# Nine matmuls of ones in TensorE's order for each of the first three pairs of attention tiles

## The chip, the cores and the metric

The kernel runs on one core of one Trainium2 chip. The metric is the device time of one execution in microseconds (us); the median over runs is what two kernels are compared by.

## The reference, cut to what matters

Pooled attention over 2 batches of 8 heads, then two feed-forward blocks on the 1152 tokens that come out. Inputs and outputs are float32.

```python
q_pool = q.reshape(B, H, S // 2, 2, D).mean(axis=3)           # B, H, S, D = 2, 8, 1152, 64
scores = (1 / sqrt(D)) * q_pool @ k^T
attn = exp(scores - max); attn = attn / (sum(attn) + 1e-9)
x = attn @ v                                                   # reshaped to 1152 x 512
h = x @ w_in;  g = P(h) / (Q(h) + 1e-6);  x = g @ w_out        # w_in 512 x 2048
xn = rms_norm(x) * rms_g
out = (silu(xn @ w_gate) * (xn @ w_val)) @ w_out2              # w_gate, w_val 512 x 1536
```

## The kernel before, in words

**Attention** goes by pairs of heads. A pair of heads has nine tiles of 128 pooled queries (four of the first head, one that holds the last 64 queries of both, four of the second head); the eight pairs of heads make 72 tiles. For one tile, QK is the score matmuls of line 783 into three PSUM banks of `hid`, in two pieces, AB (banks 0 and 1) and C (bank 2). DVE takes the negated row maximum (line 812), ACT the exponentials with their sums (line 818), PE turns them (line 834) back into the same banks, piece T and, once the copy of bank 0 has left, piece T2; ACT and DVE copy the turned tile into `pt` (lines 866 and 869). When all tiles of a head are there, PE multiplies `pt` with the values (line 938, into `av`). There are two sets of banks, one for even tiles and one for odd ones, so QK of a tile waits until the tile two before it has been copied out.

**What comes beside it.** For each head, K and the pooled Q (the sum of line 674, on POOL or DVE) are turned on PE (line 732, into `prep`) and copied to `kT` and `qT` (lines 616 and 619). When a pair of heads is finished, its rows are divided by their sums (lines 989 and 994) and split into a rounded part `x_hi` (lines 616 or 619) and a rest `x_lo` (line 632). During attention the float64 weights of the first feed-forward block are also loaded and turned into float32 pairs: the first nine stay in SBUF (lines 175 to 208), the later ones, here called spills, go through ACT (175, 215), DVE (180, 223) and POOL (219, 232, 236) and back to DRAM.

**The order on PE** is written out in `attention()`, in the list `seq`. It takes tiles two by two: AB and C of both, then up to five value products of earlier tiles, then T of both, then T2 of the first. Each entry of `seq` depends on the one before it. The value products come from `av_ops`; the first of them carries the number 4 (the tile that completes the first head), and one is taken only in turns with a larger tile number, so the turns of tiles 0 and 1, 2 and 3, 4 and 5 have none.

**The order elsewhere** comes from a planner, `order()`. It holds a list of operations with costs in nanoseconds, buffers and due times, steps through a modelled time, and for each engine picks among what is ready; an operation that has several ways (a copy by ACT or DVE, a sum by POOL or DVE) gets the one that ends first by the model. The instructions are issued in the order that comes out, and at run time they wait for each other by semaphores. SP issues all DMAs, in one queue.

**Before the first QK**, `f_warm` issues nine matmuls of `ones` by `ones` (line 1015).

The feed-forward blocks follow (the matmuls of line 525). Their first two units of hidden features are projected while attention ends, and the rational function of the first block (lines 1125 to 1176) reads the projections out of the same `hid` banks: a bank set is free again when DVE has done line 1134 for it.

Of the kernel before, what the change touches and what calls it, by code (L numbers as in the profile page):

```python
# [8 lines left out]
F32 = mybir.dt.float32  # L9
# [5 lines left out]
PSUM = bass.MemoryType.PSUM  # L15
# [4 lines left out]
def attention_moe_moe2_kernel(  # L20
# [18 lines left out]
    nc = tc.nc  # L39
# [19 lines left out]
    def pool(tag, bufs=1, space=None):  # L59
        if tag not in pools:  # L60
            kw = {} if space is None else {"space": space}
            pools[tag] = scope[-1].enter_context(tc.tile_pool(name=tag, bufs=bufs, **kw))
# [3 lines left out]
    def T(tag, shape, dtype=F32, space=None):  # L66
        pool(tag, BUFS.get(tag, 1), space)
        return pools[tag].tile(shape, dtype, tag=tag, name=tag)
# [5 lines left out]
    ones = T("ones", [128, 128])  # L74
# [369 lines left out]
    PE, DVE, ACT, POOL = "PE", "DVE", "ACT", "POOL"  # L444
# [89 lines left out]
    def banked(accesses, g, ins, also=None):  # L534

        ins = ins.ins
        for o in range(3):
            for other in accesses[o]:
                if other.engine != ins.engine:
                    if o != g and other is not also:  # L540
                        tc.declare_no_dep(ins, other, reason="another bank")
                    else:
                        tc.add_manual_dep(ins, other.name, after, reason="the same bank")
        accesses[g].append(ins)
# [64 lines left out]
    TS = 3100  # L609
# [284 lines left out]
    LAST = [NFULL, 2 * NFULL]  # L894
# [117 lines left out]
    def f_warm():  # L1012

        for _ in range(WARM):
            banked(bank[0], 0, nc.tensor.matmul(s_ps[0][:, 0, 0:128], lhsT=ones, rhs=ones, start=True, stop=True))

    WARM = 9

    tile_pe, av_ops = {}, []
    AV2 = 5  # L1020

    def attention():
        Op(PE, 213 * WARM, -1e6, f_warm)
        for i in range(len(heads)):
            head_ops(i)
        for i in range(NP * NT):
            tile_ops(i)
            if i % NT == NT - 1:
                pair_ops(i // NT)


        seq = []
        n = NP * NT
        for i in range(0, n, 2):
            a, b = tile_pe[i], tile_pe[i + 1]
            was = tile_pe.get(i - 1)
            seq += [a["AB"], *([was["T2"]] if was else []), a["C"], b["AB"], b["C"]]
            for _ in range(AV2):
                if av_ops and av_ops[0][0] < i - AVLAG:
                    seq.append(av_ops.pop(0)[1])  # L1040
            seq += [a["T"], b["T"], a["T2"]]
        seq.append(tile_pe[n - 1]["T2"])
        for x, y in zip(seq, seq[1:]):
            y.deps.append(x)

    AVLAG = 0

    attention()
    later = sum_op[0][4]
    early_h = {}  # L1050
# [475 lines left out]
```

## Time and profile before

| | us |
|---|---|
| median of 3 runs | 716.89 |
| lowest and highest run | 714.22 and 717.25 |
| the profiled execution, its own time | 718.36 |
| its span, first to last instruction | 716.6 |
| PE busy | 689.0 (96%) |
| DVE busy | 546.1 (76%) |
| ACT busy | 397.6 (55%) |
| POOL busy | 258.6 (36%) |
| mean granted clock of TensorE | 0.990 |

The span is cut into 40 slices of 17.9 us in the page's view of busy shares. Attention fills the first 15 or so (to about 278 us), the first feed-forward block the next 12, the second the rest. PE means TensorE's matmuls, DVE VectorE, ACT ScalarE, POOL GpSimdE, SP the engine that issues DMAs. A float32 matmul of the program stands as two entries in the trace, a transpose as one. [...]

### The profile page before, as it was taken

The numbers are of one execution on the slowest core, as the hardware profiler recorded it, in microseconds if no ns is written. First come the engines' busy times: TensorE is split into PE (matmuls) and PEld (weight loads), VectorE is DVE, ScalarE is ACT, GpSimd is POOL, SyncE is SP. The second block draws the span as 40 slices with busy tenths as digits, with TensorE's granted clock in tenths as the row PEclk, the third lists the DMA queues.
The fourth block names the chain that finished last, engine by engine and source line by source line (L and its number), as shares of the span: only waits on it lengthen the run. The fifth ranks groups of instructions, "written<-read, shape, count | busy, mean of one in ns | idle before, by whom it ended". The sixth has DMA issues, their size and how long they took to land.

```text
span 716.6 us, 13077 instructions
## 1 busy us (share of the span) xinstructions
PE 689.0 (96%) x5257; PEld 596.5 (83%) x5257; DVE 546.1 (76%) x721; ACT 397.6 (55%) x630; POOL 258.6 (36%) x240
## 2 busy tenths in 40 slices
PE   7999999999999999899999999998999999999997
PEld 6666666667666677899999999997999899989996
DVE  5599998989898885997996967957768156845844
ACT  4568776878877875977755655344334232402210
POOL 3022334656654465312221323255345033403500
PEclk9799999999999999999999999999999999999999
DMA  6443434765554535214105104000225112420103
GB/s 209 113 133 119 124 96 156 223 192 180 202 168 143 190 120 202 93 59 146 60 30 171 36 2 149 28 29 0 89 89 148 60 59 83 125 89 29 59 1 132
DMA packets 53900, 77.66 MB, mean 108 GB/s; under 512 B 6480, under 2 KB 36176, under 8 KB 53840
## 3 DMA queue, kind: packets, MB, share of 16 engines
q1 hardware_dynamic: 53840, 76.83, 33.3%
q8 instruction: 41, 0.67, 0.4%
q14 instruction: 19, 0.16, 0.1%
HBM read 62.40 MB, written 14.42 MB: 107 GB/s over the span
## 4 chain that ended last, share of the span: by engine, by line
PE 81%; DVE 12%; ACT 4%; issue 2%; DMA 0%; SPq 0%; DVEq 0%; ACTq 0%
PE hid L525 32%; PE accp L525 23%; PE hid L783 9%; PE av L938 9%; PE hid L834 5%; DVE nm L812 2%; DVE pt L869 2%; ACT p L818 2%; PE prep L732 2%; DVE acc L1324 1%; DVE xt L619 1%; DVE m_q L1141 1%; PE prep L985 1%; DVE wc L184 1%; DVE x_lo L1334 0%
## 5 line engine op out<-in xcount | busy, mean ns | idle before, releaser
L525 PE MATMUL hid<-x_hi,win_hi 128*128 128x384 f32 x480 | 162.3, 338 | 3.6 <-DVE m_p L1134 1.4
L525 PE MATMUL hid<-x_lo,win_hi 128*128 128x384 f32 x480 | 161.2, 336 | 0.6 <-DVE x_lo L1334 0.6
L525 PE MATMUL hid<-x_hi,win_lo 128*128 128x384 f32 x480 | 161.1, 336 | 0.0
L818 ACT ACTIVATE p<-hid,nm 128x1152 f32<-128x1152 f32 x72 | 87.9, 1222 | 28.2 <-DVE nm L812 28.0
L812 DVE TENSOR_REDUCE nm<-hid 128x1 f32<-128x1152 f32 x72 | 94.9, 1353 | 10.2 <-PE hid L783 8.9
L525 PEld LDWEIGHTS hid<-x_hi,win_hi 128*128 128x128 f32 x480 | 90.7, 189 | 6.7 <-issue 3.5
L783 PE MATMUL hid<-kT,qT 64*128 64x256 f32 (+3 forms) x800 | 95.2, 379 | 0.8 <-DVE pt L869 0.4
L1176 POOL TENSOR_TENSOR g_lo<-m_p,g_hi 128x1152 fp32r<-128x1152 f32 (+1 forms) x20 | 44.5, 2233 | 135.2 <-ACT g_hi L1173 96.8
L525 PEld LDWEIGHTS hid<-x_lo,win_hi 128*128 128x128 f32 x480 | 90.6, 189 | 1.8 <-DVE x_lo L1334 0.9
L525 PEld LDWEIGHTS hid<-x_hi,win_lo 128*128 128x128 f32 x480 | 90.5, 189 | 0.0
L834 PEld LDWEIGHTS hid<-ident,p 64*128 64x128 f32 x1296 | 53.6, 141 | 37.7 <-ACT p L818 12.3
L834 PE MATMUL hid<-ident,p 64*128 64x64 f32 x1296 | 68.5, 232 | 12.2 <-ACT p L818 7.0
L783 PEld LDWEIGHTS hid<-kT,qT 64*128 64x128 f32 (+1 forms) x800 | 70.5, 182 | 9.0 <-DVE pt L869 1.3
L938 PE MATMUL av<-pt,vn 128*64 128x288 f32 x576 | 76.7, 411 | 0.0
L866 ACT ACTIVATE pt<-hid 128x512 f32<-128x512 f32 (+2 forms) x145 | 59.7, 449 | 29.8 <-PE hid L834 29.3
L525 PE MATMUL accp<-g_hi,wout_hi 128*128 128x384 f32 x192 | 64.8, 337 | 3.0 <-ACT acc L1229 1.8
L525 PE MATMUL accp<-g_hi,wout_lo 128*128 128x384 f32 x192 | 64.2, 334 | 0.0
L525 PE MATMUL accp<-g_lo,wout_hi 128*128 128x384 f32 x192 | 64.2, 334 | 0.0
L938 PEld LDWEIGHTS av<-pt,vn 128*64 128x64 f32 x576 | 38.7, 136 | 27.1 <-issue 3.4
L175 ACT ACTIVATE wc<-wraw 128x512 f32<-128x512 f32 x68 | 45.4, 671 | 26.5 <-POOL win_lo L208 14.7
L869 DVE COPY pt<-hid 128x512 f32<-128x512 f32 (+1 forms) x79 | 47.6, 608 | 16.4 <-PE hid L834 14.9
L203 POOL TENSOR_SCALAR win_hi<-wc 128x512 fp32r<-128x512 f32 x22 | 15.2, 691 | 99.8 <-PE hid L525 90.8
(120 smaller groups left out, 1236.2 us busy)
## 6 DMA issues: line engine op xcount, KB each, us to landing
wraw<-in_moe_w_out_dram SPq DMA_DIRECT2D x28, 512.0 KB, 3.4
far<-spill SPq DMA_DIRECT2D x23, 512.0 KB, 3.3
wraw<-in_moe_w_in_dram SPq DMA_DIRECT2D x16, 512.0 KB, 3.8
wraw<-in_moe_w_gate_dram SPq DMA_DIRECT2D x12, 512.0 KB, 3.8
wraw<-in_moe_w_val_dram SPq DMA_DIRECT2D x12, 512.0 KB, 4.2
kn<-in_k_dram SPq DMA_DIRECT2D x16, 288.0 KB, 3.9
vn<-in_v_dram SPq DMA_DIRECT2D x16, 288.0 KB, 3.1
qn<-in_q_dram SPq DMA_DIRECT2D x16, 256.0 KB, 3.3
```

What stands on the lines that cost most here:

```text
L175: nc.scalar.activation(c.bitcast(F32), wt["raw", n][:, :, 1].bitcast(F32), AF.Abs, scale=2.0**-112)
L203: eng.tensor_scalar(hi, w_float(n), 1.0, 1.0, op0=ALU.mult, op1=ALU.mult)
L525: ins = nc.tensor.matmul(dst, lhsT=a[x], rhs=b[y], start=first and i == 0 and p == 0, stop=last and i == n - 1 and p == 2,)
L732: seen(nc.tensor.transpose(ps[:, at:at + 128], src, ident))
L783: ins = nc.tensor.matmul(ps[to, j, c:c + x1 - x0], lhsT=qT[2 * pr + h][rows, c0:c0 + to.stop - to.start], rhs=kT[2 * pr + h][rows, x0:x1], ...
L812: nc.vector.tensor_reduce(out=e["nm"], in_=scores(), op=ALU.max, axis=AX.X, negate=True)
L818: nc.scalar.activation(e["p"], scores(), AF.Exp, bias=e["nm"], scale=1.0, accum_out=sums[pr][:, t:t + 1])
L834: ins = nc.tensor.transpose(ps[:, g, c:c + 64], e["p"][rows, 128 * j:128 * j + 128], ident[rows, rows])
L866: return nc.scalar.activation(to, src, AF.Copy)
L869: return nc.vector.tensor_copy(to, src)
L938: nc.tensor.matmul(e["av", h][64 * c:64 * c + 64, 0:QW], lhsT=v_tile[2 * pr + h][:, KEYS[kt], :], rhs=pt[pr, h][:, kt, c * QW:(c + 1) * QW ...
L1176: eng.tensor_sub(g_(1), p_(), g_(0).bitcast(F32))
```

## The change

A function `f_fill` issues nine matmuls of `ones` by `ones` into a buffer of `av` that nobody reads. In `attention()` one such operation is put into `seq` behind C of the second tile of a turn, as long as no value product has been taken yet: that is the turns of tiles 0 and 1, 2 and 3, and 4 and 5. Its cost for the planner is 9 times 213 ns.

```diff
+    def f_fill():
+        ps = T("av", [128, 512], F32, space=PSUM)
+        for _ in range(FILL):
+            nc.tensor.matmul(ps[:, 0:128], lhsT=ones, rhs=ones, start=True, stop=True)
+
-    WARM = 9
+    WARM, FILL = 9, 9
...
             for _ in range(AV2):
                 if av_ops and av_ops[0][0] < i - AVLAG:
                     seq.append(av_ops.pop(0)[1])
+            if av_ops[0][0] == LAST[0] and len(seq) < 40 and seq[-1] is b["C"]:
+                seq.append(Op(PE, 213 * FILL, i * TS, f_fill, [], [Buf("av")]))
             seq += [a["T"], b["T"], a["T2"]]
```

The planner sees later times on PE from the first turn on, and so other engines' orders move as well. Two places follow.

The start of PE's order, first turn, as a piece of the difference (`hid` holds the scores, `av` the filling, `prep` the turned K and Q of the second head, `p` the exponentials):

```order
 L783 MATMUL hid<-kT_197,qT_213 128x256 x4
 L783 MATMUL hid<-kT_197,qT_213 128x128
+L1020 MATMUL av<-ones 128x128 x9
 L732 MATMUL prep<-ident,kn 128x128
 L732 MATMUL prep<-ident,qp 128x128 x3
```

The filling stands ahead of four transposes of the second head. The same in the second turn:

```order
 L783 MATMUL hid<-kT_197,qT_213 128x256 x4
 L783 MATMUL hid<-kT_197,qT_213 128x128
+L1020 MATMUL av<-ones 128x128 x9
 L834 MATMUL hid<-ident,p 128x64 x35
 L783 MATMUL hid<-kT_197,qT_213 64x256
```

Here it stands directly ahead of the turning of tiles 2 and 3; in the third turn it stands ahead of four transposes of the third head.

DVE in the same stretch, before (`pt` is the turned tile, `nm` the negated maximum, `qp` the pooled query of a head):

```order
L619 TENSOR_SCALAR kT_232<-prep 128x128
L619 TENSOR_SCALAR qT_277<-prep 128x384
L869 COPY pt<-hid 128x8x64
L619 TENSOR_SCALAR qT_277<-prep 128x256
L869 COPY pt<-hid 128x8x64
L812 TENSOR_REDUCE nm<-hid 128x1 x2
```

and with the change:

```order
L619 TENSOR_SCALAR kT_232<-prep 128x128
L619 TENSOR_SCALAR qT_309<-prep 128x384
L869 COPY pt<-hid 128x8x64
L619 TENSOR_SCALAR qT_309<-prep 128x256
L674 TENSOR_TENSOR qp<-qn_153 128x640
L869 COPY pt<-hid 128x8x64
L812 TENSOR_REDUCE nm<-hid 128x1 x2
```

The sum that makes the fourth head's pooled query has come from POOL's queue into DVE's, ahead of the copy of tile 1 and of the maxima of tiles 2 and 3.

The end of attention on DVE, before (`xt` is the last pair of heads' result, `m_q` and `m_p` the first block's rational function; after the change the lines behind 1040 have numbers seven higher):

```order
L223 SCALAR_TENSOR_TENSOR wc<-wraw,wc 128x512
L989 TENSOR_TENSOR xt<-xt,prep 128x512
L619 TENSOR_SCALAR x_hi<-xt 128x576
L632 TENSOR_TENSOR x_lo<-xt,x_hi 128x576
L1141 SCALAR_TENSOR_TENSOR m_q<-m_u,absb,hid 128x384
```

and with the change:

```order
L223 SCALAR_TENSOR_TENSOR wc<-wraw,wc 128x512
L180 TENSOR_SCALAR wc<-wc 128x512
L223 SCALAR_TENSOR_TENSOR wc<-wraw,wc 128x512
L989 TENSOR_TENSOR xt<-xt,prep 128x512
L994 TENSOR_TENSOR xt<-xt,rxh 64x64 x2
L632 TENSOR_TENSOR x_lo<-xt,x_hi 128x576
L1148 SCALAR_TENSOR_TENSOR m_q<-m_u,absb,hid 128x384
```

One spill more is worked on here, the division of the last columns (line 994) has come from POOL to DVE, and `x_hi` has gone to ACT, where it stands ahead of the rational function's first operation (line 1125 before). POOL has its three operations of the additional spill (219, 232, 236) where line 994 stood. Between these two places DVE's queue takes up the first weight one turn earlier (four of its operations stand ahead of the maxima of tiles 8 and 9), and around tiles 32 to 42 the parts of the division move from DVE to POOL in one pair of heads; PE's order changes there by a few transposes that stand behind QK instead of in the midst of it.

## Rows read from the trace of the kernel before

**Rows 1.** Page, the span in 40 slices: granted clock in tenths
```profile
PEclk9799999999999999999999999999999999999999
```
**Rows 2.** Busy time by stretch, PE alone: window, its length, PE busy (entries), clock, DMA
```profile
18.20:18.40 0.20, 0.20 (x9) 0.82 0.93 282
...
28.40:28.60 0.20, 0.20 (x2) 0.58 0.00 0
```
**Rows 3.** Timeline of PE, first 30 us: start, length, operation, entries [idle before, releaser]
```profile
1.04 3.99 PE L1015 MATMUL hid<-ones 128*128 128x128 f32 x18 [1.04 <-DVE ones L75]
...
7.39 2.22 PE L783 MATMUL hid<-kT,qT 64*128 64x256 f32 x20
...
11.54 0.77 PE L834 MATMUL hid<-ident,p 64*128 64x64 f32 x17 [1.34 <-ACT p L818]
...
17.72 0.80 PE L834 MATMUL hid<-ident,p 64*128 64x64 f32 x17 [1.91 <-ACT p L818]
18.98 1.22 PE L834 MATMUL hid<-ident,p 64*128 64x64 f32 x18 [0.46 <-ACT p L818]
20.14 1.98 PE L783 MATMUL hid<-kT,qT 64*64 64x256 f32 x16
...
22.34 3.12 PE L783 MATMUL hid<-kT,qT 64*64 64x128 f32 x14
25.39 1.11 PE L732 MATMUL prep<-ident,kn 128*128 128x128 f32 x4
...
28.63 0.78 PE L834 MATMUL hid<-ident,p 64*128 64x64 f32 x18
```
**Rows 4.** Timeline of PE, a later turn with the same 14 entries
```profile
154.61 1.72 PE L783 MATMUL hid<-kT,qT 64*64 64x128 f32 x14
```
**Rows 5.** Timeline of all engines, first 20 us
```profile
5.06 0.83 DVE L674 TENSOR_TENSOR qp<-qn 128x640 f32<-128x640 f32 x1 [3.42 <-DMA qn<-in_q_dram]
...
13.63 0.69 DVE L869 COPY pt<-hid 128x512 f32<-128x512 f32 x1 [0.24 <-PE hid L834]
...
14.33 1.53 POOL L674 TENSOR_TENSOR qp<-qn 128x640 f32<-128x640 f32 x1 [1.00 <-DMA qn<-in_q_dram]
...
14.96 2.62 DVE L812 TENSOR_REDUCE nm<-hid 128x1 f32<-128x1152 f32 x2 [0.64 <-PE hid L783]
...
16.36 1.22 ACT L818 ACTIVATE p<-hid,nm 128x1152 f32<-128x1152 f32 x1 [1.39 <-DVE nm L812]
```
**Rows 6.** Timeline of DVE, maxima of tiles 8 and 9
```profile
37.68 2.62 DVE L812 TENSOR_REDUCE nm<-hid 128x1 f32<-128x1152 f32 x2
```
**Rows 7.** Timeline of DVE, POOL and PE, 124 to 130 us
```profile
125.20 1.73 DVE L632 TENSOR_TENSOR x_lo<-xt,x_hi 128x576 fp32r<-128x576 f32 x1
...
124.93 1.39 POOL L219 TENSOR_TENSOR wc<-wc,wraw 128x512 f32<-128x512 f32 x1 [6.11 <-ACT pt L866]
...
129.60 0.77 PE L834 MATMUL hid<-ident,p 64*128 64x64 f32 x17
```
**Rows 8.** Timeline of POOL, DVE and PE, end of attention
```profile
275.14 1.28 POOL L219 TENSOR_TENSOR wc<-wc,wraw 128x512 f32<-128x512 f32 x1
...
277.21 1.29 POOL L236 TENSOR_TENSOR spill<-wc,spill 128x512 fp32r<-128x512 f32 x1
...
278.56 0.69 DVE L989 TENSOR_TENSOR xt<-xt,prep 128x512 f32<-128x512 f32 x1 [4.51 <-ACT xt L616]
...
279.85 0.76 DVE L632 TENSOR_TENSOR x_lo<-xt,x_hi 128x576 fp32r<-128x576 f32 x1
280.52 0.61 DVE L1141 SCALAR_TENSOR_TENSOR m_q<-m_u,absb,hid 128x384 f32<-128x384 f32 x1
...
286.06 0.41 PE L525 MATMUL hid<-x_hi,win_hi 128*128 128x384 f32 x1 [1.42 <-DVE m_p L1134]
```
**Rows 9.** Timeline and stretches of PE, first feed-forward block
```profile
303.88 0.45 PE L525 MATMUL accp<-g_hi,wout_hi 128*128 128x384 f32 x1 [1.76 <-ACT acc L1229]
...
306.00:308.00 2.00, 2.00 (x8) 0.50 0.35 116
```

## Prediction

> **What bounds the kernel now.** I read the page's slices first. The granted clock is full everywhere but in the first slice and, far lower, in the second [rows 1]; the busy shares there show attention's first turns. A finer cut of PE's time gives the edges: the clock falls within 18.2 to 18.4 us and is back within 28.4 to 28.6 [rows 2], so some 10 us run at the lower level. What went before is in PE's timeline: PE is idle 1.34 us before tile 0 is turned and 1.91 us before tile 2 is, both times for ACT's exponentials [rows 3], because no value products stand there yet. From 18.98 us (turning of tile 3) to 28.63 (turning of tile 5) the chain of waits names PE alone: 9.65 us in which PE is what everything waits for. The same 14 matmuls cost 3.12 us there and 1.72 in a later turn at the full level [rows 3, 4], a ratio of 1.8. Later attention is held by PE and DVE by turns, the change of stage by DVE, and from about 305 us on PE has hardly a gap. So a microsecond that PE gains or loses before 305 mostly reaches the end, unless the other engines take it.
>
> **Price of one filling.** The trace has the same nine matmuls once, at the start: 18 entries in 3.99 us [rows 3]. That would be 3.99 us each in the turns if they had run at full speed, which is what the clock column prints there. I don't believe the column: an entry of 128 columns took 0.22 us, while the 14 entries of the later turn, 128 to 256 columns wide, took 0.12 each [rows 4]. If line 1015 ran at the lower level, the ratio 1.8 gives 2.2 us, a plain halving 2.0. I take 2.1, with ends 2.0 and 3.99.
>
> [...] By the printed column each of the three costs 1.9 more, up to 5.7 us on the sum below. [...]
>
> **First turn.** QK of tile 1 ends at 9.61, 7.39 + 2.22 [rows 3]. The filling runs to 11.7, four transposes behind it (about 0.6 at full speed: 1.11 over 1.8 [rows 3]) to 12.3, and tile 0 is turned 0.75 us later than the 11.54 of before; 1.34 of the 2.1 lie in the idle time. Then DVE: the sum of line 674 now stands ahead of the copy of tile 1. On POOL it waited for its queries to land, until 14.33 [rows 5], and the load's issue isn't moved. So DVE stands until 14.33, sums (0.83), copies (0.69), and the maxima of tile 2 begin at 15.85 instead of 14.96: +0.9. Ends: +0.5 if the data come earlier, +1.1 if the sum takes longer.
>
> **Second turn.** QK of tile 3 waits for that copy and ends near 17.0; the filling runs to 19.1. The exponentials of tile 2 are ready at about 15.85 + 1.4 + 1.3 = 18.6 (half of 2.62, and 1.22 with its hand-over [rows 5]), of tile 3 at 19.9. Tile 2 is turned from 19.1 to 19.8, tile 3 from 19.95 instead of 18.98: +1.0. So two fillings and the moved sum have cost 1.0 us, and PE's longest idle time up to there is about 0.9 us.
>
> **Third turn, where the clock pays.** At the full level I count from 19.95: turning 0.7 [rows 3], 16 QK entries 1.1 (1.98 over 1.8), one transpose 0.15, 14 entries 1.6 (1.72 less what overlaps) [rows 4], the third filling 2.1, transposes 0.6, turning 0.7, transposes 0.6: 7.5 us, so tile 5 is turned at 27.4 instead of 28.63. **The start gains 1.2 us.** Without the filling the list is 5.4, but the chain of maxima and exponentials of tiles 4 and 5 takes over (QK of tile 4 done at 18.98 + 0.7 + 1.1 + 0.4 = 21.2, then 1.35 + 1.35 + 1.3), and tile 5 couldn't start before 25.2: the most that the clock can give is 28.63 − 25.2 = 3.4, less the shift. Ends of the whole start: −2.5 and +0.5.
>
> **Turn of tiles 8 and 9.** Four weight operations now stand on DVE before the maxima that begin at 37.68 [rows 6]. Two fit in DVE's gaps there, one delays a copy that isn't last; the subtraction that waits for POOL's rounding delays the maxima by up to one operation of 0.7 us, and PE has value products to do. +0.3, ends 0 and 0.7.
>
> **Tiles 32 to 42.** Where division, rounding and rest left DVE for POOL, DVE's maxima at 126.86 stood behind a rest of 1.73 us [rows 7]. DVE loses over 2 us of work ahead of them, but PE turned the next tile at 129.60 with no idle time worth a bracket, so PE's own list hides most of it. −0.4, ends −1.5 and +0.8 for the rest of the shuffle.
>
> **End of attention.** One spill more for POOL: from 275.14 to 278.50 one takes 3.4 us [rows 8], so the new one fills 278.5 to 281.9. DVE and POOL hold each other up: the rest of line 632 took 1.73 us beside POOL's product of 1.39 [rows 7], and 0.76 alone [rows 8]; it ended 0.6 after POOL's product did, so it waited for it. In the new order line 994 (DVE, from 279.2) meets POOL's product until 279.8, `x_hi` goes to ACT and back (0.7 with hand-overs), and the rest starts near 281, beside POOL's last subtraction, and ends near 282.6 instead of 280.6. Behind it on DVE stand all of the rational function's operations, and PE, idle 1.42 us at 286.06 for DVE to free a bank [rows 8], would wait about 3.4. **This gives back 2.0 us.** Ends: +0.3 (POOL's last spill runs elsewhere) and +2.6.
>
> **Sum.** −1.2 + 0.3 − 0.4 + 2.0 = +0.7 on an execution of 718.36, which makes 719.1. That execution lies 1.5 above the median of the runs shown, so I forecast **717.6 us** beside a median of 716.89: no change that can be told, since about 0.5% (3.6 us) is what a measurement of this kernel can tell from none.
>
> **Rivals.**
> - The clock falls all the same. Place: the turns of tiles 0 to 5. It decides at whether PE stays at the full level through the 0.9 us wait for the moved sum and through 18.2 us. Against it: PE is busier than before in each of these microseconds. For it: at 303.88 PE had waited only 1.76 us and the clock was at 0.50 soon after [rows 9]. Then the shift of 1.0 stays, nothing is gained, and the third filling lies wholly on PE's path at 4.0 us: +5.0 in place of −1.2, sum +6.9, **723.8 us**, slower. Chance 0.07.
> - The last spill doesn't meet line 632 on POOL, because POOL keeps its old pace or DVE gets in first. Then the end of attention costs 0.3 and the sum is −1.0: **715.9**. For it: POOL's times are rough. Chance 0.22; not told from no change.
> - PE's longer wait at the end of attention lets the clock fall there, as it did behind the 1.76 us. The stretch there lasted about 3.4 us, so half of it, 1.7, is added: **719.3**. Chance 0.13, and with the upper ends of the other terms it is the rest of what can be slower.
> - The fillings hide and the moved sum doesn't wait: the start gives −2.5, the middle −1.5, the end +0.3: −3.7, **713.2**, faster. Against it: the bracket on POOL's sum names the load. Chance 0.07.
>
> **How the numbers follow.** The forecast has 0.51 of the chance. With the second and third rivals its time lies between 714 and 721: the terms' ends taken together reach −3.7 and +4.6, but hardly all at once, and the runs of before alone spread from 714.22 to 717.25. The range 714.0 to 720.8 leaves out the first and last rivals and the outer ends. Faster by over 0.5%: the last rival, 0.07. Slower: the first, and 0.05 from the third with bad ends, 0.12. Same: 0.81.
>
> **What would show it.** Right: the clock column at full in the second slice; no idle bracket on PE at 10 to 12 and 16 to 18 us, one of some 0.9 before QK of tile 3; 18 entries of line 1020 in about 2.1 us three times; tile 5 turned near 27.4; line 632's last instance at well over 0.76 us beside POOL's line 236; PE's first wait for line 1134 (now 1141) over 2.5 us. Wrong: the clock still at 0.50 around 20 to 28 us, fillings of 4 us, or an end of attention that isn't later against its start than before.

## The result, and the profile after

| | before | with the change |
|---|---|---|
| median, first comparison | 716.55 (7 runs, 714.22 to 718.82) | 720.11 (7 runs, 718.87 to 721.64) |
| ratio, 95% interval | | 1.0058 [1.004, 1.0077] |
| second comparison, later | 716.20 (34 runs) | 719.27 (12 runs), 1.0036 [1.0018, 1.0054] |
| profiled execution, its span | 718.36, 716.6 | 721.64, 719.9 |
| mean granted clock of the profiled execution | 0.990 | 0.993 |

The change costs 3.1 to 3.6 us: slower, with both intervals above 1, by about as much as one measurement of this kernel can tell. 720.11 lies inside the forecast range (714.0 to 720.8) and 2.5 us above the forecast.

The page's slices show what the change does to the clock. The second slice, 7 before [rows 1], is full; a new dip stands in slice 17, which begins at about 288 us:

```profile
PEclk9999999999999999899999999999999999999999
```

In the timeline of PE with the change (start and length in us, entries, idle time before) the three fillings take 2.27 us each, where line 1015 took 3.99 for the same work [rows 3]:

```profile
5.05 1.27 PE L732 MATMUL hid<-ident,kn 128*128 128x128 f32 x5
...
8.00 2.22 PE L783 MATMUL hid<-kT,qT 64*128 64x256 f32 x20
10.15 2.27 PE L1020 MATMUL av<-ones 128*128 128x128 f32 x18
...
17.34 2.28 PE L1020 MATMUL av<-ones 128*128 128x128 f32 x18
...
20.48 0.91 PE L834 MATMUL hid<-ident,p 64*128 64x64 f32 x18 [0.16 <-ACT p L818]
...
24.20 2.27 PE L1020 MATMUL av<-ones 128*128 128x128 f32 x18
...
28.28 0.78 PE L834 MATMUL hid<-ident,p 64*128 64x64 f32 x18
```

Tile 5 is turned at 28.28 instead of 28.63 [rows 3]. The first QK began 0.61 later (8.00 against 7.39). That differs from execution to execution: the queries arrived 0.25 us later here, and the five transposes at 5.05 took 1.27 us where they took 0.71 before. Counted from the first QK, the turning of tile 5 comes 20.28 us later instead of 21.24. So against the profiled execution of before the start gains 0.96.

The end of attention with the change, all engines (lines 1141 and 1148 are 1134 and 1141 of before):

```profile
277.96 0.69 DVE L989 TENSOR_TENSOR xt<-xt,prep 128x512 f32<-128x512 f32 x1 [0.83 <-ACT xt L616]
278.25 1.30 POOL L219 TENSOR_TENSOR wc<-wc,wraw 128x512 f32<-128x512 f32 x1
278.56 1.76 DVE L994 TENSOR_TENSOR xt<-xt,rxh 64x64 f32<-64x64 f32 x2
...
280.34 1.29 POOL L236 TENSOR_TENSOR spill<-wc,spill 128x512 fp32r<-128x512 f32 x1
...
280.42 0.69 ACT L616 ACTIVATE x_hi<-xt 128x576 fp32r<-128x576 f32 x1 [2.49 <-DVE xt L994]
281.14 1.10 DVE L632 TENSOR_TENSOR x_lo<-xt,x_hi 128x576 fp32r<-128x576 f32 x1 [0.81 <-ACT x_hi L616]
...
282.31 0.61 DVE L1148 SCALAR_TENSOR_TENSOR m_q<-m_u,absb,hid 128x384 f32<-128x384 f32 x1
...
288.06 0.66 PE L525 MATMUL hid<-x_hi,win_hi 128*128 128x384 f32 x1 [3.58 <-DVE m_p L1141]
```

From line 989 to the first `m_q` it takes 4.35 us where it took 1.96 [rows 8], and PE, which waited 1.42 us [rows 8], waits 3.58. Towards the end of that wait the clock, which is given in shares of full speed, falls to 0.50, and it stays there until 294 (the clock records of both profiles, of before and with the change, hold 0.50 and 1.00 and no other level). The stretches of PE (window, length, busy (entries), clock, DMA share, GB/s):

```profile
284.00:286.00 2.00, 0.48 (x3) 1.00 0.96 298
286.00:288.00 2.00, 0.00 (x0) 0.79 0.96 332
288.00:290.00 2.00, 1.94 (x6) 0.50 1.06 385
290.00:292.00 2.00, 2.00 (x7) 0.50 0.94 304
292.00:294.00 2.00, 2.00 (x8) 0.50 0.00 1
294.00:296.00 2.00, 2.00 (x13) 1.00 0.00 0
```

### The profile page after: what moved, and what is told of

Same layout as the page of the kernel before. It is cut to its first block, busy times and chain, and to the rows that moved or that the text cites. A ratio compares the mean times of both kernels' runs of the same rounds, so it can differ in the third digit from the quotient of the medians.

```text
span 719.9 us, 13185 instructions
## 1 busy us (share of the span) xinstructions
PE 694.6 (96%) x5311; PEld 604.1 (84%) x5311; DVE 548.8 (76%) x723; ACT 395.9 (55%) x627; POOL 258.4 (36%) x241
## 4 chain that ended last, share of the span: by engine, by line
PE 81%; DVE 12%; ACT 4%; issue 2%; DMA 1%; DVEq 0%; ACTq 0%
PE hid L525 32%; PE accp L525 23%; PE av L938 8%; PE hid L783 8%; PE hid L834 5%; DVE pt L869 3%; PE prep L732 2%; ACT p L818 2%; DVE nm L812 2%; DVE acc L1331 1%; DVE xt L619 1%; DMA wraw<-in_moe_w_out_dram 1%; PE av L1020 1%; PE hid L1015 1%; DVE m_q L1148 1%
## 5 line engine op out<-in xcount | busy, mean ns | idle before, releaser
L783 PE MATMUL hid<-kT,qT 64*128 64x256 f32 (+3 forms) x800 | 92.6, 370 | 0.9 <-DVE pt L869 0.7
```

The source lines that it names most:

```text
L783: ins = nc.tensor.matmul(ps[to, j, c:c + x1 - x0], lhsT=qT[2 * pr + h][rows, c0:c0 + to.stop - to.start], rhs=kT[2 * pr + h][rows, x0:x1], ...
```

## The experiments

My theory after this comparison: the fillings gain at the start, and the planner's new orders lose more at the end of attention. Rivals: the fillings themselves cost, or the low clock behind 288 us makes the difference.

**All fillings, the old orders.** The filling costs the planner nothing and takes no buffer, so every other instruction stands where it stood before.

```diff
-                seq.append(Op(PE, 213 * FILL, i * TS, f_fill, [], [Buf("av")]))
+                seq.append(Op(PE, 0, i * TS, f_fill))
+                seq[-1].mode = "rows"
```

> The three fillings stand on PE, but the planner counts them as nothing, so every other engine keeps the order of before. Theory (the fillings gain about 1 us, and the moved orders at the end of attention lose it threefold): the clock stays at full through the second slice, the maxima of tiles 8 and 9 begin 0.5 to 1.5 us earlier than in before, PE waits 1.4 us for line 1134's bank as before, and the time is 1 to 2 us under before (ratio 0.997 to 0.999). Rival (the fillings themselves cost, 2.1 us each on PE's path): 2 to 4 us over before, with no difference at the end of attention.

Measured: 717.05 (12 runs; 715.60 for the 35 runs of before beside them), ratio 1.0011 [0.9991, 1.0031]: between theory and rival. Most of the change's loss is gone, and PE waits 1.41 us at the end of attention, as before. But no gain came; the theory's first half failed. Yet this profile has the clock at 1.00 from 9 to 30 us, as wanted.

**The new orders without the fillings.**

```diff
     def f_fill():
-        ps = T("av", [128, 512], F32, space=PSUM)
-        for _ in range(FILL):
-            nc.tensor.matmul(ps[:, 0:128], lhsT=ones, rhs=ones, start=True, stop=True)
+        pass
```

> The planner counts the fillings, but none is issued: the orders of the change without its matmuls. Theory: the clock falls to 0.50 near 18 us as in before, the start loses what the moved sum of line 674 costs (0 to 1 us), the end of attention shows PE's wait of 3 to 4 us for DVE, and the time is 3.5 to 5.5 us over before (ratio 1.005 to 1.008), slower than the change itself by about 1. Rival (the fillings themselves cost): within 1 us of before.

Measured: 719.93, ratio 1.0045 [1.0023, 1.0067], a little less than expected. The orders alone cost about what the change costs (1.0058 and 1.0036). PE waits 3.38 us at the end of attention, and the clock falls there too; timeline and stretches of PE:

```profile
286.75 0.41 PE L525 MATMUL hid<-x_hi,win_hi 128*128 128x384 f32 x1 [3.38 <-DVE m_p L1139]
```
```profile
286.00:288.00 2.00, 1.25 (x7) 1.00 1.02 374
288.00:290.00 2.00, 2.00 (x9) 0.51 1.09 372
290.00:292.00 2.00, 2.00 (x9) 0.64 0.39 124
```

**Two fillings, the old orders.** The first of these kernels, with the third turn's filling left out (`and i < 4` in the condition).

> As with the old orders, but the third filling (behind tile 5) is left out. Theory: if the clock stays at full with two fillings, the third's 2.1 us are no longer on PE's path, tile 5 is turned near 25.5 us, and the time is 2 to 3.5 us under before (ratio 0.995 to 0.997). If the clock falls within 18 to 28 us all the same, it is within 1 us of before: then the third filling is needed for the clock.

Measured: 716.26, ratio 0.9995 [0.9974, 1.0015], 0.8 below three fillings on the same chip, with intervals that overlap. The forecast of 0.995 to 0.997 was missed although the clock is at 1.00 from 18 to 30 us: tile 5 is turned at 27.10 and not near 25.5, since without the third filling PE waits 1.00 us for the exponentials of tile 4. From the first QK to the turning of tile 5 it takes 18.89 us (8.21 to 27.10) against 20.02 with three (8.44 to 28.46): the third filling lies on PE's path by half of its 2.27 us.

**The last spill behind the last line 632.** The change with the three GpSimd operations of its last spill held back; all orders else are the change's.

```diff
-        nc.gpsimd.tensor_mul(c, c, wt.pop(("raw", n))[:, :, 1].bitcast(F32))
+        ins = nc.gpsimd.tensor_mul(c, c, wt.pop(("raw", n))[:, :, 1].bitcast(F32))
+        if n == SPILL[-1]:
+            tc.add_manual_dep(ins.ins, rest_ins[-1].name, after, reason="behind the last rest")
```

> The change, with every engine's order as it is, but POOL's three operations of the last spill wait until DVE has done the last line 632. Theory (POOL's spill holds DVE's lines 994 and 632 back, PE waits, and the clock falls there): line 994 takes about 0.45 us instead of 1.76, line 632 0.76 instead of 1.10, the first m_q of line 1148 begins 1.5 to 1.8 us earlier, PE's wait is near 1.9 us, and the time is 2 to 3.5 us under the change, near before (ratio to before 0.999 to 1.002). Rival (it is the way over ACT, line 616 for x_hi, or the clock for another reason): lines 994 and 632 are quicker, but PE's wait stays over 3 us and the time within 1 us of the change (ratio 1.005 to 1.007).

Measured: 718.24, ratio 1.0031 [1.0013, 1.0048]. The change itself, measured beside other runs of before, has 1.0058 and 1.0036, so what this gives back can't be read well from the times; the timeline is clearer (this kernel's 1002, 1007, 624 and 642 are 989, 994, 616 and 632 of the change):

```profile
277.84 0.69 DVE L1002 TENSOR_TENSOR xt<-xt,prep 128x512 f32<-128x512 f32 x1 [0.84 <-ACT xt L624]
278.45 0.44 DVE L1007 TENSOR_TENSOR xt<-xt,rxh 64x64 f32<-64x64 f32 x2
278.99 0.69 ACT L624 ACTIVATE x_hi<-xt 128x576 fp32r<-128x576 f32 x1 [1.17 <-DVE xt L1007]
279.71 0.76 DVE L642 TENSOR_TENSOR x_lo<-xt,x_hi 128x576 fp32r<-128x576 f32 x1 [0.81 <-ACT x_hi L624]
280.55 1.31 POOL L219 TENSOR_TENSOR wc<-wc,wraw 128x512 f32<-128x512 f32 x1 [2.39 <-DVE x_lo L642]
...
286.70 0.41 PE L533 MATMUL hid<-x_hi,win_hi 128*128 128x384 f32 x1 [2.75 <-DVE m_p L1154]
```

With POOL out of the way the division's rest takes 0.44 instead of 1.76, the subtraction 0.76 instead of 1.10, and PE's wait falls to 2.75 us; in this profile the clock is 1.00 from 286 to 294 us. The wait lies between theory (near 1.9) and rival (over 3). That DVE was held up beside POOL is shown; that POOL was isn't: its product takes 1.30 us in the change and 1.31 here. From line 1002 to PE's release it takes 8.86 us, against 10.10 with the change and 7.50 before: somewhat under half of what this stretch lost comes back. The rest comes from elsewhere than this meeting.

**The kernel before, profiled again.** Fillings that held the clock and gained nothing left one doubt: whether the slow second slice of the recorded profile is the kernel's habit. The unchanged kernel was profiled twice more.

> The kernel before, unchanged, profiled once more. Theory: the ten slow microseconds at the start of the recorded profile (mean clock 0.990) were a matter of that execution, and most executions of the kernel before have little of them. Then the mean clock is 0.995 or more, the granted clock between 18 and 30 us is over 0.8 instead of 0.57, and from the first QK matmul of tile 0 to the turning of tile 5 it takes 18 to 19.2 us instead of 21.2. Rival: the slow stretch belongs to the kernel. Then the clock is 0.6 or less there again and the distance is about 21 us.

> The same once more, since one execution can be of either kind. Theory: mean clock 0.995 or more, 18 to 19.2 us from the first QK matmul to the turning of tile 5. Rival: 0.990 and 21 us.

Measured: 715.54 and 715.63, mean clock 0.996 both times. From the first QK to the turning of tile 5: 19.55 and 19.47 us, a little over the 18 to 19.2 expected, and far from 21.24. Timeline and stretches of PE in the first:

```profile
7.66 2.22 PE L783 MATMUL hid<-kT,qT 64*128 64x256 f32 x20 [0.25 <-ACT qT L616]
...
17.99 0.77 PE L834 MATMUL hid<-ident,p 64*128 64x64 f32 x17 [1.91 <-ACT p L818]
19.25 1.22 PE L834 MATMUL hid<-ident,p 64*128 64x64 f32 x18 [0.49 <-ACT p L818]
...
22.61 1.72 PE L783 MATMUL hid<-kT,qT 64*64 64x128 f32 x14
...
27.21 0.78 PE L834 MATMUL hid<-ident,p 64*128 64x64 f32 x18
```
```profile
18.00:19.00 1.00, 0.76 (x17) 1.00 0.68 193
19.00:20.00 1.00, 0.75 (x14) 0.61 0.38 90
20.00:21.00 1.00, 1.00 (x18) 0.50 0.52 71
21.00:22.00 1.00, 1.00 (x16) 0.50 0.84 199
22.00:23.00 1.00, 1.00 (x11) 0.68 1.00 295
23.00:24.00 1.00, 1.00 (x11) 1.00 0.89 313
```

The same 1.91 us of waiting, the same fall, but the clock is back after 3.4 us instead of the 10.2 of the recorded execution [rows 2], and the 14 entries take 1.72 us instead of 3.12 [rows 3]. The runs of before that stood beside the experiments show how the mean clock and the time go together:

| mean clock of the run | runs of 92 | us |
|---|---|---|
| 0.988 to 0.990 | 18 | 718.72 to 720.74 |
| 0.994 and 0.995 | 23 | 716.47 to 717.61 |
| 0.996 to 0.998 | 37 | 715.03 to 716.30 |
| 0.999 and 1.000 | 14 | 713.94 to 714.74 |

The recorded profile of before, 718.36 at 0.990, belongs by its clock to the slowest fifth. An estimate from these traces: 3.4 us at 0.50 take 0.0024 from the mean clock of a span of 714 us. So the first group spends some 14 us or more at the lower level, the last about 2 us at most; in the last group the clock can have fallen behind the wait at 18 us only briefly, if at all. Where the low stretches of the timed runs lie isn't shown.

**The change, with ones in PE's wait at the end of attention.**

```diff
+        if u == 2:
+            def f_fill2():
+                ps = acc_psum()
+                for _ in range(14):
+                    nc.tensor.matmul(ps[:, 0:128], lhsT=ones, rhs=ones, start=True, stop=True)
+
+            Op(PE, 0, -1e6, f_fill2)
         ps, done = early_h.pop(u) if u in early_h else project_ops("in", u, key)
```

> The changed kernel with 14 more matmuls of ones (about 3.5 us) in PE's wait of 3.58 us at the end of attention, every other instruction in the same order. Theory: the clock's fall at 288 us comes from that wait. Then the clock is 1.00 from 286 to 300 us, the executions at a mean clock of 0.993 (721.5 us) are gone, and the median is 0.5 to 1.5 us below that of the change, 718.6 to 719.6. Rival: the wait isn't what lets the clock fall, or the ones themselves hold up what follows. Then the median stays at 720 to 721 and executions at 0.993 remain.

Measured: 720.12, ratio 1.0033 [1.0015, 1.0051]. Timeline and stretches of PE:

```profile
284.27 3.29 PE L1103 MATMUL accp<-ones 128*128 128x128 f32 x28
287.82 0.41 PE L525 MATMUL hid<-x_hi,win_hi 128*128 128x384 f32 x1 [0.26 <-DVE m_p L1148]
```
```profile
286.00:288.00 2.00, 1.74 (x15) 1.00 0.94 325
288.00:290.00 2.00, 2.00 (x13) 1.00 1.07 390
```

Half a hit. The clock stays at 1.00, no run has a mean clock under 0.998 (of the change's 19 runs, 7 have 0.995 or less), and from PE's release to the end of its next long wait it takes 17.98 us instead of 19.31. But the median isn't under the change's two (720.11 and 719.27). So the fall at 288 us is what the wait costs in addition in some executions, not what makes the typical one slow. Five of these runs lie at a mean clock of 0.999 or 1.000 and take 718.58 to 719.29.

**Fillings cut to fit.** The old orders, five ones in the first turn, seven in the second, none in the third; run twice, on two chips.

```diff
-    WARM, FILL = 9, 9
+    WARM, FILL = 9, {0: 5, 2: 7}
```

> The kernel before with five matmuls of ones in the first turn, seven in the second, none in the third; all other orders as before. Theory: nine were longer than PE's idle time in these turns (1.34 and 1.9 us), and what stuck out cost 0.6 to 1 us. Then the distance from the first QK matmul to the turning of tile 5 is 18.0 to 18.9 us with the clock at 1.00, and the median is 0.3 to 0.8 us below the 716.26 of two fillings of nine, 715.4 to 716.0, with no execution over 718. Rival: the short fillings leave gaps in which the clock falls. Then it is at 0.50 for some microseconds between 18 and 30 us, and the median is 716.3 or more.

> Five and seven ones in the first two turns, again, on another chip, since the first interval touched 1. Theory: it saves what the ordinary execution of before loses at the start, about 1.4 us. Median 1.0 to 1.7 us below that of before, ratio 0.9965 to 0.999. Rival: no difference, ratio 0.999 to 1.001.

Measured: 715.34, ratio 0.9979 [0.9957, 1.0001], and 714.68, 0.9980 [0.9963, 0.9997]. Timeline of PE in the second:

```profile
8.28 2.22 PE L783 MATMUL hid<-kT,qT 64*128 64x256 f32 x20 [0.26 <-ACT qT L616]
10.43 1.38 PE L1020 MATMUL av<-ones 128*128 128x128 f32 x10
...
12.43 0.77 PE L834 MATMUL hid<-ident,p 64*128 64x64 f32 x17 [0.18 <-ACT p L818]
...
16.63 1.83 PE L1020 MATMUL av<-ones 128*128 128x128 f32 x14
18.60 0.78 PE L834 MATMUL hid<-ident,p 64*128 64x64 f32 x17
...
26.41 0.78 PE L834 MATMUL hid<-ident,p 64*128 64x64 f32 x18
```

Tile 0 still waits for its exponentials (0.18), so the filling delays nothing, and tile 5 is turned 18.13 us after the first QK: 1.4 less than in the ordinary execution of before, 2.1 less than with the change. This version beats the kernel before by 0.2%, with one of its two intervals touching 1, and the change by 4.6 us on the chip that they share (714.68 against 719.27). One run of its 24 is above 717 (719.20, at 0.995), where none over 718 was expected.

Runs of equal mean clock say what the fillings themselves cost. At 0.999 and 1.000 they take:

| | such runs | us |
|---|---|---|
| before | 14 of 92 | 713.94 to 714.74 |
| five and seven ones | 15 of 24 | 713.86 to 715.39 |
| two fillings of nine | 5 of 12 | 714.88 to 715.23 |
| three fillings of nine, old orders | 6 of 12 | 716.12 to 716.63 |

The fitted fillings don't make the fastest executions faster; they make them common. Three fillings of nine cost about 2 us there: so the rival that the fillings themselves cost was partly right, and the clock that they hold pays for most of it in the typical execution (20.02 us to the turning of tile 5 against the ordinary 19.55).

**Seven ones in the second turn alone** (the condition with `i == 2`).

> Seven ones in the second turn alone, all else as before. Theory: the clock falls behind the second turn's wait of 1.9 us, and the first turn's 1.34 us do no harm. Then the clock is 1.00 from 18 to 30 us in the profile, it takes 18.0 to 18.6 us from the first QK matmul to the turning of tile 5, and the median is within 0.4 us of that of five and seven. Rival: the first turn's wait counts as well. Then the clock is at 0.50 for some microseconds between 12 and 30 us, and the median lies at or above that of before less 0.5.

Measured: 716.91, ratio 1.0009 [0.9984, 1.0035]. The profile is as the theory had it (clock 1.00 from 18 to 30 us, 18.13 us to the turning of tile 5), but that was one execution at 0.998; 5 of the 12 have 0.995 or less and take 717.8 to 720.7. The median went against the theory, as the rival had it: by it the first filling is worth having. Where the clock fell in those five runs wasn't seen.

**The change with its end as before**: the last pair's division rest on GpSimd, `x_hi` on VectorE, the last spill behind line 632.

```diff
+                [...][:1 if pr == NP - 1 else 2],
...
+        o_xh = op_any(xh_ways[1:2] if pr == NP - 1 else xh_ways, key + 2000, o_div, [xb])
```

> The changed kernel with the last pair's end as before: the rest of the division on GpSimd, x_hi on VectorE, and the last spill's three GpSimd operations behind the last line 632. Theory: what the last spill kept back after it was moved (718.24) is the way over ScalarE. Then from line 989 to the first m_q it takes about 2.0 us instead of 3.0 (and 4.35 in the change), PE's wait is near 1.5 us, and the median is 0.7 to 1.3 us below 718.24, at 717.0 to 717.6, level with the change's fillings in the old order (717.05). Rival: the loss comes from the shuffle of the weights' work earlier or later in the kernel. Then it stays at 718 or more.

Measured: 720.29, ratio 1.0050 [1.003, 1.0071]: a miss. Timeline:

```profile
277.79 0.69 DVE L1002 TENSOR_TENSOR xt<-xt,prep 128x512 f32<-128x512 f32 x1 [0.85 <-ACT xt L624]
...
279.96 0.61 DVE L1165 SCALAR_TENSOR_TENSOR m_q<-m_u,absb,hid 128x384 f32<-128x384 f32 x1
...
286.12 0.41 PE L533 MATMUL hid<-x_hi,win_hi 128*128 128x384 f32 x1 [2.24 <-DVE m_p L1158]
...
294.47 0.44 PE L533 MATMUL accp<-g_hi,wout_hi 128*128 128x384 f32 x1 [1.87 <-ACT g_hi L1197]
295.61 0.58 PE L533 MATMUL accp<-g_lo,wout_hi 128*128 128x384 f32 x1 [0.69 <-POOL g_lo L1200]
```

Stretch of PE behind these waits:

```profile
294.00:300.00 6.00, 4.84 (x17) 0.72 0.29 104
```

The way to the first `m_q` is short again (2.17 us), but PE still waits 2.24 us for its bank, and then 1.87 and 0.69 more for `g`, where the clock falls too. From its release to the end of its wait of 1.76 us it takes 21.25 us instead of 18.02 to 19.31 with the change. Those two waits are new: the rational function's operations still stand in the order that the planner made for the later start, and on SP one load of a later weight now stands behind four others that it stood ahead of. The time that one place gave back was lost behind it. How much of that is the order on ACT and DVE, how much the moved load and how much the clock stays open.

**The change once more**, beside these three.

> The changed kernel once more, beside the next three on one chip. Theory: its loss is no matter of the first chip. Then the ratio is 1.004 to 1.007 again, and the executions fall into those at a mean clock of 0.998 or more (719 to 720) and those that lost the clock at 288 us (0.993 to 0.995, 721 to 722). Rival: the first comparison was drawn from few runs, and the ratio is under 1.003.

Measured: 719.27, 1.0036 [1.0018, 1.0054], between theory and rival. Its profile lies at 0.998 and has the same 3.58 us of waiting, with 3.4 us at 0.50 behind it instead of 6.8.

## Why the prediction came out as it did

The time lies in the range by the room that the range left for bad ends and the third rival, not by the sum: +0.7 was worked out and 3.1 to 3.6 measured. The mechanisms were mostly right; the size of the start and of the end of attention was not.

The steps side by side, in us from landmark to landmark; "ordinary" is the first repeated profile of before.

| step | before, recorded | before, ordinary | change, recorded | change again |
|---|---|---|---|---|
| start of the program to the first QK | 7.39 | 7.66 | 8.00 | 7.94 |
| to the turning of tile 5 | 21.24 | 19.55 | 20.28 | 20.27 |
| to line 989 of the last pair | 249.93 | 249.95 | 249.68 | 249.67 |
| to PE's release at the end of attention | 7.50 | 7.51 | 10.10 | 10.10 |
| to the end of PE's wait of 1.76 us | 17.82 | 17.80 | 19.31 | 18.02 |
| to the end of the span | 412.72 | 411.33 | 412.53 | 411.20 |

**Price of one filling: right.** 2.1 forecast, 2.27 measured; the clock column's 1.00 over line 1015 was rightly not believed. The trace's clock records begin only at 4.7 us in the recorded execution of before and at 7.3 us with the change, and up to there the entries are slow; the 1.00 printed ahead of them stands for no record. The nine matmuls took 3.99 us at the start of the program, 0.22 an entry, and 2.27 in the turns, 0.13 an entry at a recorded clock of 1.00.

**First three turns: right against the recorded profile, wrong as a forecast.** Turns of tiles 0, 2 and 3 moved as worked out, except that the moved sum of line 674 found its data there: no wait on DVE, and 0.16 us of idle time on PE before tile 3. The gain was 0.96 of the 1.2 forecast. The step that failed stands in the first paragraph and in the sum: "some 10 us run at the lower level", taken for the kernel's own and then merely shifted by the 1.5 us that the execution lay above the median. (The paragraph's reading of [rows 1] is too broad as well: the first slice is as full as the others, and the 3.4 us at 0.50 of [rows 9] are too short to show in a slice.) In the ordinary execution the low stretch lasts 3.4 us, and the change loses 0.7 there (20.28 against 19.55). The sign was to be had: 718.36 was above all three timed runs (highest 717.25), and the one oddity in its profile was the stretch that the change was to remove.

**Turn of tiles 8 and 9, tiles 32 to 42.** Forecast −0.1 together, measured −0.25. Right.

**End of attention: right in mechanism, mis-sized by 0.6.** 2.0 forecast, 2.6 measured (10.10 against 7.50), with PE's wait at 3.58 for about 3.4. DVE's work took longer beside POOL's: 1.76 us for line 994 beside line 219 and 0.44 with POOL out of the way, 1.10 for line 632 beside line 236 and 0.76. By what POOL holds DVE up isn't shown. Of the 2.6, holding the spill back returned 1.24; what makes the rest isn't shown.

**The rival of the falling clock came true beside the forecast**, not in place of it. It was priced at 1.7; the recorded execution paid 1.5 (19.31 against 17.82), the repeated one 0.2. I gave it 0.13; both profiles of the change show the fall (6.8 us at 0.50 and 3.4), and 7 of its 19 runs have a mean clock of 0.995 or less. As a rival it excluded the forecast; it should have been a term with a chance.

**The other rivals.** The clock didn't fall in the turns of tiles 0 to 5; the last spill did meet line 632; the fillings didn't hide.

Added up against the ordinary execution: +0.3 for the first QK, +0.7, −0.3, +2.6, +0.2 to +1.5, and −0.1 to +1.2 for the later fall, is +3.4 (717.2 − 713.8) to +6.1 (719.9 − 713.8); the +0.3 is the executions' and not the change's. The larger part of the loss comes from the orders, which moved because the planner was told of the fillings. With the orders left alone the same nine ones three times took 717.05; cut to PE's idle time they gain. The runs at a mean clock of 0.999 or 1.000 say the same: from three fillings in the old orders to the change with its end filled they rise from 716.12–716.63 to 718.58–719.29, by 2.5 to 2.7, which is what the end of attention lost.

## What to carry to other kernels

Before a change is priced by a stretch of one profile, compare that execution's time with the timed runs: if it lies above them all, what is odd in it may be its own, and the gain from removing it is paid out only in the executions that have it. Where the clock differs between executions, compare runs of equal mean clock: they tell a filling's cost from its gain. A filling that keeps the clock up should be cut to the idle time it stands in (here ratios of 0.9979 and 0.9980 against 1.0011 with three of nine), and hidden from a planner whose orders it would shift: here the shifted orders cost more (1.0045 alone) than the clock gave. Undoing one place of a written-out order didn't restore the old time here (1.0050), since all that follows was ordered for the new one.

## What the runs showed that I had not expected

The clock didn't answer the same wait in the same way. Behind the wait of 1.91 us at 18 us it stayed low for 10.2 us once and for about 3.4 us twice. Behind the wait of 1.76 us in the first feed-forward block it fell in 9 of 14 profiles (0.50 for 3.4 us each time, as [rows 9]) and stayed at 1.00 in 5, among them both repeated profiles of before. Nor did the length of a wait decide it here: behind waits of 2.24 and 2.75 us (one profile each) it held. The spread of this kernel's time, 713.94 to 720.74 over 92 runs, goes in step with the mean clock, and no two groups of the table overlap. No run here shows what makes the answers unequal, and why low stretches last 3.4, 6.8 or 10.2 us stays open.
